# Zero products at the opening of a retention and rational feed-forward kernel: 59 of 64 columns and 3 long ones, in place of 93 in quarters of the array and 4 long ones

## The chip, the cores and the metric

The kernel runs on one core of a Trainium2 chip. The metric is the device time of one execution, in microseconds (us); smaller is better. Three runs of the kernel before are known: median 615.11 us, 614.29 to 615.46.

## What is computed

A retention layer (linear attention with a decaying state) feeds a feed-forward layer whose activation is a quotient of two polynomials. Cut to what matters:

```python
# q, k, v: (4, 8, 768, 64); w_in: (512, 2048); w_out: (2048, 512); a: 4 numbers, b: 2 numbers
gamma = 1.0 - 2.0 ** (-5.0 - np.arange(H))
for t in range(S):
    state = gamma[None, :, None, None] * state + np.einsum('bhd,bhe->bhde', k[:, :, t], v[:, :, t])
    y[:, :, t] = scale * np.einsum('bhd,bhde->bhe', q[:, :, t], state)
x = y.transpose(0, 2, 1, 3).reshape(B * S, H * D)          # 3072 x 512
h = x @ w_in
P = a[0] + a[1] * h + a[2] * h**2 + a[3] * h**3
Q = 1.0 + abs(b[0]) * abs(h) + abs(b[1]) * h**2
out = (P / (Q + 1e-06)) @ w_out
```

The zero products of this case are no part of it: TensorE multiplies a tile of zeros into a PSUM bank that nobody reads.

## The kernel before, in words

**Tiling.** The retention is done in chunks of 128 tokens: 4 batches by 6 chunks are 24 chunks. The first chunk of each batch (`first_chunk`, four calls) needs no state: its scores (`first_scores`, tile `pa`, L352) are k by q, VectorE multiplies them by the decay mask (tile `aT`, L541), and `first_values` (tile `px`, L358 and L366) multiplies by v. ScalarE and VectorE then split the result into a rounded high part and a rest (`xh`, L470, and `xl`, L474), since the large matrix products run as three products of such parts. The feed-forward layer goes over 6 blocks of 512 tokens and 16 slices of 128 hidden columns, 96 slots. In a slot TensorE makes `ph` (L827, 12 products of 512 columns), ScalarE, VectorE and GpSimd work out the quotient in some ten instructions, and TensorE adds to `po` (L846, 12 products).

**Weights.** They arrive as 64 bit numbers in 32 tiles `raw` of 512 KB each. `decode` turns each into a high part and a rest: two ScalarE instructions (tile `t`, L786, and tile `u`, L790), two on VectorE (L796, L799), a copy on ScalarE (L805) and a subtraction on GpSimd (L808). The first 16 or so are decoded while the first slots run.

**Order.** A planner written in the kernel (class `Plan`) orders all steps ahead of time from tables of costs and ranks; every engine then runs its list strictly in that order, and all loads and stores go through the one queue of SyncE (SP, L315) in that order. At most eight transfers are under way at once.

**The zeros.** When the planner finds a gap of over 0.7 us on TensorE, it puts zero products there. `fill` makes the long ones: 128 rows, 128 columns of weights, 512 columns streamed, bfloat16 (L291). Ahead of the very first step of TensorE, and only there, `open_with` runs (L303): 93 products of fp32 zeros, 64 by 64 weights and 16 streamed columns, by turns in two quarters of the array (`r = half(i % 2)` picks rows and output partitions 0 to 63 or 64 to 127); it then sets the number of long ones that follow, `BEGINNING`, to 4. The numbers do not enter the planner's times: it has fixed the order already when `open_with` runs. The tile `zeros` is a VectorE memset at the program's start (L259). The first step after the opening is the scores of one first chunk, then three long zeros, the scores of a second one, four long zeros, and the values of both.

Of the kernel before, what the change touches and what calls it, by code (L numbers as in the profile page):

```python
# [8 lines left out]
F32 = mybir.dt.float32  # L9
# [194 lines left out]
def tile_retention_rational_ffn(  # L204
# [22 lines left out]
    H, D = kk.shape[3], kk.shape[4]  # L227
# [26 lines left out]
    zeros = const.tile([P, P], BF16, name="zeros")  # L254
# [42 lines left out]
    def open_with(bank):  # L297


        few_ = zeros.bitcast(F32)  # L300
        for i in range(TURNING):
            r = half(i % 2)
            nc.tensor.matmul(  # L303
                bank[r, :16], few_[r], few_[r, :16], start=True, stop=True, skip_group_check=True
            )
        spare[0] = BEGINNING

# [19 lines left out]
    def half(x):  # L327
        return slice(x * D, (x + 1) * D)
# [704 lines left out]
    with tc.manual_schedule(  # L1033
# [45 lines left out]
        def emit(x, engine, gap):  # L1079

            nonlocal idle
            if engine == "PE" and zeros_for(gap):
                spare[0] = zeros_for(gap)
                if not begun(1):
                    if idle is None:
                        idle = ps.tile([P, TB], F32, name="idle", tag="b1")
                        open_with(idle)
                    fill(idle, True)
                elif open_po:
                    fill(open_po[0], False)  # L1090
            x.run(engine)
            spare[0] = 0
# [262 lines left out]
ENDING = (  # L1355
    (0, 0), (1, 0), (0, 1), (1, 1), (0, 2), (2, 0), (2, 1), (1, 2), (2, 2), (0, 3), (1, 3), (2, 3),
)
TURNING = 93
BEGINNING = 4


_ARRAYS = (
# [100 lines left out]
```

## Time and profile before

| | |
|---|---|
| median of 3 runs | 615.11 us (614.29 to 615.46) |
| the profiled execution | 615.57 us |
| its span, first to last instruction | 613.9 us |
| TensorE busy (products) | 605.4 us, 99% of the span |
| TensorE weight loads | 494.5 us, 81% |
| VectorE busy | 442.3 us, 72% |
| ScalarE busy | 429.8 us, 70% |
| GpSimd busy | 330.3 us, 54% |
| all DMA | 59.45 MB |

The profile is of one execution. PE stands for TensorE's products, PEld for its weight loads, DVE for VectorE, ACT for ScalarE, POOL for GpSimd, SPq for the DMA queue of SyncE. The zero products count as busy, so 99% says nothing of useful work. Of 615.57 us, 1.7 lie outside the span.

### The profile page before, as it was taken

The page shows a single profiled execution, that of the slowest core. Times are in us where ns is not written, and L with a number is a line of the kernel's source. Part 1 is how long each engine was busy: PE and PEld are TensorE (multiplying, and loading weights), DVE is VectorE, ACT ScalarE, POOL GpSimd, SP SyncE. Part 2 cuts the span into 40 slices and gives each one's busy share as a digit, 9 for nine tenths or more (in the row PEclk, how much of TensorE's full clock was granted, in tenths as well). Part 3 has the DMA queues.
Part 4 walks back from the last instruction along what each step waited for, and adds up shares of the span by engine and source line. Part 5 has one row for each costly group of instructions (what it writes and reads, how often), then busy time and mean ns, then how long its engine had stood idle before and what let it go on. Part 6 is the DMA issues. An engine that isn't in the chain of part 4 may idle for free.

```text
span 613.9 us, 13176 instructions
## 1 busy us (share of the span) xinstructions
PE 605.4 (99%) x5358; PEld 494.5 (81%) x5358; DVE 442.3 (72%) x665; ACT 429.8 (70%) x699; POOL 330.3 (54%) x276
## 2 busy tenths in 40 slices
PE   9998999999999999999999999999999999999997
PEld 7766888888888888888888888888888888888885
DVE  0699999898878868766677766666776666766664
ACT  1599989999855655756675775576775667777663
POOL 0478778786865655445544544444454344444442
PEclk9999999999999999999999999999999999999999
DMA  9999931001222470705003300400231000100001
GB/s 315 321 383 407 369 107 68 2 0 69 57 64 105 144 236 21 222 8 167 2 1 124 118 1 18 156 1 1 87 106 51 1 1 1 69 0 1 0 2 68
DMA packets 30412, 59.45 MB, mean 97 GB/s; under 512 B 3216, under 2 KB 8592, under 8 KB 30352
## 3 DMA queue, kind: packets, MB, share of 16 engines
q1 hardware_dynamic: 30352, 58.61, 26.9%
q8 instruction: 42, 0.69, 0.4%
q14 instruction: 18, 0.15, 0.1%
HBM read 50.21 MB, written 8.39 MB: 95 GB/s over the span
## 4 chain that ended last, share of the span: by engine, by line
PE 89%; DVE 0%; ACT 0%; issue 0%
PE po L846 42%; PE ph L827 41%; PE px L422 3%; PE pa L392 2%; PE pk L401 2%; DVE p L938 0%; DVE t L799 0%; DVE ph L937 0%; DVE q L936 0%; ACT o L993 0%
## 5 line engine op out<-in xcount | busy, mean ns | idle before, releaser
L909 POOL TENSOR_TENSOR q<-q,s 128x512 f32<-128x512 f32 x96 | 124.2, 1294 | 185.1 <-ACT s L898 170.3
L827 PE MATMUL ph<-xh,w 128*128 128x512 f32 (+2 forms) x776 | 208.3, 390 | 2.7 <-DVE p L938 1.4
L846 PE MATMUL po<-w,gh 128*128 128x512 f32 x768 | 199.5, 392 | 0.0
L827 PEld LDWEIGHTS ph<-xh,w 128*128 128x128 f32 x776 | 143.7, 188 | 33.7 <-ACT w L805 2.1
L846 PEld LDWEIGHTS po<-w,gh 128*128 128x128 f32 x768 | 143.0, 188 | 30.3
L936 DVE SCALAR_TENSOR_TENSOR q<-q,small,ph 128x512 f32<-128x512 f32 x96 | 71.7, 746 | 112.3 <-ACT ph L925 111.8
L948 POOL TENSOR_TENSOR gl<-p,gh 128x512 fp32r<-128x512 f32 x96 | 124.4, 1296 | 36.6 <-ACT gh L944 19.7
L924 ACT ACTIVATE s<-q,small 128x512 f32<-128x512 f32 x96 | 69.5, 724 | 64.9 <-POOL q L909 64.9
L846 PE MATMUL po<-w,gl 128*128 128x512 f32 x384 | 110.4, 390 | 0.0
L889 ACT ACTIVATE q<-ph 128x512 f32<-128x512 f32 x96 | 57.4, 598 | 69.3 <-PE ph L827 68.7
L827 PE MATMUL ph<-xl,w 128*128 128x512 f32 (+2 forms) x388 | 103.3, 388 | 0.0
L827 PEld LDWEIGHTS ph<-xl,w 128*128 128x128 f32 x388 | 72.6, 188 | 15.2
L846 PEld LDWEIGHTS po<-w,gl 128*128 128x128 f32 x384 | 72.0, 188 | 15.3 <-POOL gl L948 0.3
L904 ACT ACTIVATE p<-ph,small 128x512 f32<-128x512 f32 x96 | 74.5, 776 | 0.0
L918 DVE SCALAR_TENSOR_TENSOR p<-p,small,ph 128x512 f32<-128x512 f32 x96 | 71.7, 747 | 3.4
L917 DVE TENSOR_TENSOR p<-ph,p 128x512 f32<-128x512 f32 x96 | 65.7, 685 | 8.8 <-ACT p L904 8.4
L937 DVE SCALAR_TENSOR_TENSOR ph<-p,small,ph 128x512 f32<-128x512 f32 x96 | 71.9, 749 | 0.0
L938 DVE SCALAR_TENSOR_TENSOR p<-q,ph 128x512 f32<-128x512 f32 x96 | 65.9, 687 | 3.3
L944 ACT CAST gh<-p 128x512 fp32r<-128x512 f32 x96 | 59.1, 616 | 12.2 <-DVE p L938 12.0
L898 ACT ACTIVATE s<-q,small 128x512 f32<-128x512 f32 x80 | 65.0, 812 | 0.1
L925 ACT ACTIVATE ph<-s 128x512 f32<-128x512 f32 x96 | 57.8, 602 | 4.2 <-DVE p L918 0.9
L808 POOL TENSOR_TENSOR w<-t,w 128x512 fp32r<-128x512 f32 x32 | 41.4, 1297 | 30.4 <-ACT w L805 30.3
(59 smaller groups left out, 434.1 us busy)
## 6 DMA issues: line engine op xcount, KB each, us to landing
v<-in_v SPq DMA_DIRECT2D x34, 256.0 KB, 4.7
raw<-in_w_in SPq DMA_DIRECT2D x16, 512.0 KB, 9.0
raw<-in_w_out SPq DMA_DIRECT2D x16, 512.0 KB, 8.5
qT<-in_qT SPq DMA_DIRECT2D x24, 256.0 KB, 4.7
kT<-in_kT SPq DMA_DIRECT2D x24, 256.0 KB, 4.4
k<-in_k SPq DMA_DIRECT2D x24, 256.0 KB, 4.2
out<-o SPq DMA_DIRECT2D x24, 256.0 KB, 2.3
q2T<-in_q2T SPq DMA_DIRECT2D x10, 256.0 KB, 4.8
```

The source lines that it names most:

```text
L827: nc.tensor.matmul(cell["ph"][:, t0:t1], w[0, f][:, part, kt * P : (kt + 1) * P], x[:, kt, t0:t1], start=(i == 0), stop=(i == 3 * NP - 1),)
L846: nc.tensor.matmul(o_tiles[n][tt], g_[:, tt * P : (tt + 1) * P], w[1, f][:, part], start=(first and m == 0), stop=(last and m == 2),)
L898: nc.scalar.activation(cell["s"], cell["q"], AF.Identity, bias=babs[:, 0:1], scale=babs[:, 1:2])
L904: nc.scalar.activation(cell["p"], cell["ph"], AF.Identity, bias=par_sb[:, 2:3], scale=par_sb[:, 3:4])
L909: nc.gpsimd.tensor_mul(cell["q"], cell["q"], cell["s"])
L917: nc.vector.tensor_mul(p_, ph_, p_)
L918: nc.vector.scalar_tensor_tensor(ph_ if aside else p_, p_, par_sb[:, 1:2], ph_, ALU.add, ALU.mult)
L924: nc.scalar.activation(s_, cell["q"], AF.Abs_reciprocal_sqrt, bias=qcon[:, 0:1])
L936: nc.vector.scalar_tensor_tensor(q_, q_, qcon[:, 0:1], ph_, ALU.add, ALU.mult)
L937: nc.vector.scalar_tensor_tensor(ph_, p_, par_sb[:, 0:1], ph_, ALU.add, ALU.mult)
L938: nc.vector.scalar_tensor_tensor(p_, q_, 2.0, ph_, ALU.subtract, ALU.mult, reverse0=True)
L948: nc.gpsimd.tensor_sub(cell["gl"], cell["p"], cell["gh"].bitcast(F32))
```

## The change

`open_with` makes 59 products in place of 93. Each is a bfloat16 product of 128 rows, 64 columns of weights and 64 streamed columns, always at the same place (output partitions 0 to 63), instead of an fp32 product of 64 rows, 64 columns of weights and 16 streamed columns at two places by turns. The number of long zero products behind them goes from 4 to 3. Nothing else is changed.

```diff
     def open_with(bank):
 
 
-        few_ = zeros.bitcast(F32)
         for i in range(TURNING):
-            r = half(i % 2)
             nc.tensor.matmul(
-                bank[r, :16], few_[r], few_[r, :16], start=True, stop=True, skip_group_check=True
+                bank[:D, :D], zeros[:, :D], zeros[:, :D], start=True, stop=True, skip_group_check=True
             )
         spare[0] = BEGINNING
...
-TURNING = 93
-BEGINNING = 4
+TURNING = 59
+BEGINNING = 3
```

TensorE's list before, from the program's first instruction to the first scores (`idle` is the unread PSUM bank, 64x16 and 128x512 the output):

```order
L1459 UNCONDITIONAL_BRANCH
L303 MATMUL idle<-zeros 64x16 x93
L291 LDWEIGHTS zeros
L291 MATMUL idle<-zeros 128x512
L291 LDWEIGHTS zeros
L291 MATMUL idle<-zeros 128x512
L291 LDWEIGHTS zeros
L291 MATMUL idle<-zeros 128x512
L291 LDWEIGHTS zeros
L291 MATMUL idle<-zeros 128x512
L352 MATMUL pa<-qT,kT 64x128
```

The same place of the changed kernel, from the last of its 59 pairs of weight load and product (line numbers behind the edit are two lower):

```order
L301 LDWEIGHTS zeros
L301 MATMUL idle<-zeros 64x64
L291 LDWEIGHTS zeros
L291 MATMUL idle<-zeros 128x512
L291 LDWEIGHTS zeros
L291 MATMUL idle<-zeros 128x512
L291 LDWEIGHTS zeros
L291 MATMUL idle<-zeros 128x512
L350 MATMUL pa<-qT,kT 64x128
```

The 93 products before stand without rows for their weights because fp32 products get their loads only when the program is lowered: the trace shows two passes for each, 186 loads and 186 products. From the first scores on, TensorE's list and those of the other four engines are the same as before.

## Rows read from the trace of the kernel before

**Rows 1.** Stretches: busy us of each engine, granted clock, DMA share, GB/s.

```profile
25.60:61.60 36.00, 32.94 (x443) 24.73 (x440) 33.70 (x56) 34.03 (x59) 29.34 (x26) 1.00 1.00 379
61.60:613.90 552.30, 547.97 (x4460) 450.32 (x4460) 401.17 (x592) 389.24 (x628) 297.94 (x245) 1.00 0.20 68
```

**Rows 2.** The chain that ended last, around 61 us: start, length, what.

```profile
60.77 0.70 DVE p L938
61.47 0.14 issue
61.60 0.47 PE ph L827
```

**Rows 3.** Timeline of PE's products: start, length, line, operation, count, idle time before.

```profile
0.99 10.21 PE L303 MATMUL idle<-zeros 64*64 64x16 f32 x186 [0.99 <-DVE small L261]
11.12 1.89 PE L291 MATMUL idle<-zeros 128*128 128x512 bf16 x4
12.94 1.56 PE L352 MATMUL pa<-qT,kT 64*64 64x128 f32 x32
...
15.83 1.24 PE L352 MATMUL pa<-qT,kT 64*64 64x128 f32 x32
17.00 1.04 PE L291 MATMUL idle<-zeros 128*128 128x512 bf16 x4
17.97 0.69 PE L358 MATMUL px<-aT,v 64*64 64x64 f32 x16
```

**Rows 4.** Timeline of the weight loads of the long zeros.

```profile
11.53 0.15 PEld L291 LDWEIGHTS <-zeros 128*128 128x128 bf16 x1 [0.27 <-issue]
11.96 0.15 PEld L291 LDWEIGHTS <-zeros 128*128 128x128 bf16 x1 [0.28 <-issue]
```

**Rows 5.** Line L303: weight loads, ns min/median/max, first and last start.

```profile
L303 PEld LDWEIGHTS idle<-zeros x186: 178/223/228, 1.0 to 10.9; 64*64 64x64 f32 x186
```

**Rows 6.** Tile kT, window 1.5 to 3.4 us: two loads, issued at 1.6 and 3.0.

```profile
L315 SPq DMA_DIRECT2D kT<-in_kT x2: 423/428/432, 1.6 to 3.0; - x2
...
DMA to landing us min/median/max: 4.4/4.6/4.9
```

**Rows 7.** Tile first (the masks), window 3.9 to 4.9 us.

```profile
L315 SPq DMA_DIRECT2D first<-in_mask x2: 431/432/432, 4.0 to 4.5; - x2
...
DMA to landing us min/median/max: 4.5/4.8/5.0
```

**Rows 8.** Timeline of ACT and DVE in the first 23 us.

```profile
10.84 0.75 ACT L786 ACTIVATE t<-raw,small 128x512 uint32<-128x512 uint8 x1 [2.41 <-DMA raw<-in_w_in]
...
14.55 0.56 DVE L541 TENSOR_TENSOR aT<-pa,first 128x384 f32<-128x384 f32 x1 [13.60 <-PE pa L352]
...
17.13 1.49 DVE L541 TENSOR_TENSOR aT<-pa,first 128x384 f32<-128x384 f32 x3 [2.02 <-PE pa L352]
...
19.32 0.65 ACT L470 CAST xh<-px 128x256 fp32r<-128x256 f32 x2 [7.73 <-PE px L366]
...
22.59 0.78 ACT L786 ACTIVATE t<-raw,small 128x512 uint32<-128x512 uint8 x1
```

**Rows 9.** Tile raw, window 9.4 to 9.6 us: the second weight tile.

```profile
L315 SPq DMA_DIRECT2D raw<-in_w_in x1: 432/432/432, 9.5 to 9.5; - x1
...
DMA to landing us min/median/max: 6.3/6.3/6.3
```

**Rows 10.** Tile k, window 46.5 to 47 us: the later of two loads for a pair of chunks.

```profile
L315 SPq DMA_DIRECT2D k<-in_k x1: 517/517/517, 46.8 to 46.8; - x1
...
DMA to landing us min/median/max: 6.7/6.7/6.7
```

**Rows 11.** Timeline of POOL: the two instructions that read these two k tiles.

```profile
55.18 2.04 POOL L571 TENSOR_TENSOR k<-k,small 128x512 f32<-128x512 f32 x2
```

**Rows 12.** Two more stretches, columns as in rows 1.

```profile
24.50:31.00 6.50, 6.46 (x114) 6.04 (x111) 4.56 (x11) 5.24 (x11) 4.84 (x5) 1.00 0.81 267
37.00:57.00 20.00, 19.29 (x260) 13.46 (x260) 19.43 (x31) 19.31 (x34) 18.01 (x16) 1.00 1.04 407
```

## The prediction, made before the changed kernel was run

> **What bounds the kernel now.** I read the stretches first. From 61.6 us to the end TensorE is busy 547.97 of 552.30 us [rows 1], so that part cannot get shorter by anything done at the opening; it can only begin earlier. Between 25.6 and 61.6 us VectorE and ScalarE are busy 33.70 and 34.03 of 36.00 us [rows 1]: here the decoding of the weights sets the pace, and the chain of waits says the same, since VectorE's instructions hand over to TensorE at 61.6 us [rows 2]. Both engines run fixed lists. So the question is when these lists get going.
>
> The timeline of ACT and DVE answers it. ScalarE decodes one weight tile at 10.84 us, then stands idle for 7.73 us until the first values are there, at 19.32; VectorE stands idle for 13.60 us until the first scores end, and again 2.02 us for the second [rows 8]. The instructions behind these stand in line. All of them wait for TensorE, and TensorE is busy with zeros: the quarter products from 0.99 to 11.12 us, four long ones until 12.94 [rows 3].
>
> The data is not what it waits for. The two kT tiles are issued at 1.6 and 3.0 us and land 4.4 and 4.9 us later, at 6.0 and 7.95 (the qT before each is earlier in the same queue); the masks land at 8.5 and 9.5 [rows 6, 7]. The first scores could begin 6.9 us before they do. So the length of the zero stream is on the path that sets the end, microsecond for microsecond, until another thing is late.
>
> [...]
>
> **The change, step by step.**
>
> *Out: 93 quarter products.* They take 10.21 us, 0.110 each, or 0.055 for each of the 186 pairs of load and product [rows 3].
>
> *In: 59 products of 64 columns.* No such product is in the trace. A long zero streams 512 columns in 0.43 us, so 64 columns take 0.053. A load of 64 columns should need as long; the question is whether it runs beside the product before it. Of the long zeros it does: the loads start at 11.53 and 11.96, together with the product before [rows 4]. The nearest row, the pair of load and product in the quarters, gives 0.055 [rows 3]. I take 0.055: 59 x 0.055 = 3.25 us. Bounds: at the full clock half of that, 1.6 us; in series, load then product, what a whole quarter product takes, 0.110, or 6.5 us; and if each product had to wait until the record of its load ends, 0.223 [rows 5], 13.2 us.
>
> [...]
>
> *Three long zeros instead of four.* 0.43 us less: 1.28 instead of 1.71.
>
> *Where the first scores then stand.* The zeros end at 0.99 + 3.25 + 1.28 = 5.5 us. Now the data is late next: kT at 6.0. So the first scores start near 6.05 instead of 12.94, 6.9 us earlier; half a microsecond of the saving is already a wait.
>
> *From there to the values.* The second scores stand 2.89 us behind the first (15.83 - 12.94), at 8.95, and their kT has landed. VectorE's first mask product has its mask at 8.5; the next waits for the second scores, as now. If the clock is still low, these scores end at 10.45 and the four long zeros behind them last 1.71 us instead of 0.97: the values start near 12.25, 5.7 us earlier than the 17.97 of now. If the clock rises as far behind the start of the long zeros as now (11.12 to some point between 15.83 and 17.00, so 5 us or a little more), it does so near 9.6 and the values start near 11.35, 6.6 us earlier. I take 6.1.
>
> *What of it reaches the end.* The lists of VectorE and ScalarE start 6.1 us earlier, if their inputs come. The second weight tile lands at 9.5 + 6.3 = 15.8 and is read at 22.59 [rows 8, 9], 6.8 us of slack. The tightest that I found later is the k tile issued at 46.8: it lands at 53.5, and GpSimd reads it in the second half of the pair at 55.18, at 56.2 [rows 10, 11], 2.7 us of slack. The transfers must thus move by 3.4 us as well. They can: between 24.5 and 31 us they carry 267 GB/s where 407 is had from 37 to 57 [rows 12], (1 - 267/407) x 6.5 = 2.2 us of lost time, because the queue waits for buffers that TensorE and VectorE free; they would free them earlier, and a little more is lost outside this stretch. I charge 0.2 us for what stays.
>
> *Everything else* is the same list on every engine, and 254 fewer instructions in TensorE's opening cost nothing to anyone.
>
> Sum: 615.57 - 6.1 + 0.2 = 609.7 us on the scale of the profiled execution. That one was 0.46 above the median of the runs, so I predict **609.2 us**.
>
> **The rivals.**
>
> *Load and product in series.* 59 x 0.110 = 6.5 us: the opening shrinks by 10.21 - 6.5 + 0.43 = 4.1 us, all data is there, and the time is 611.0. For it: in the quarters a product with a 16-column stream still cost 0.110. Against it: rows 4. 0.17.
>
> *The clock rises early.* If the 64-column stream raises it, as the quarter stream did not, the second scores end near 9 us, the second mask at 9.5 plus a mask product of 0.56 lets the values start near 10.1, 7.9 us earlier, and the loads, tighter by that much, take back a part, an estimate of 0.8: 7.1 us, 608.0. [...] 0.12.
>
> *The loads hold.* If the transfers do not move, only the 2.7 us of slack at the k tile are gained there: 612.4. Against it: the lost time in rows 12. 0.05.
>
> *Slower: each product waits for its own load to end.* The quarters alternate between two places and the change has one. If the next load could start only when the product before is under way, and the product only when the load's record is over, each step costs 0.178 to 0.223 us [rows 5]. At 0.18 the opening is as long as now (59 x 0.18 = 10.6 = 10.21 + 0.43) and nothing changes, 615.1; this is the point from which it decides. At 0.223 it lasts 13.2 us, 2.5 longer: 617.6. Against it: of the quarters 186 such records fit into 10.21 us, so they overlap each other. 0.04 for about the same, 0.05 for slower. A gain eaten somewhere that I did not see adds 0.02 and 0.01.
>
> **How the numbers follow.** The forecast has 0.54, and with the series, the early clock and the loads that hold, which are all faster, 0.88. Same 0.06 and slower 0.06. The bound between them is 0.2%, 1.2 us, about what a measurement of this kernel tells from no change. The range reaches from the early clock with half a microsecond to spare, 607.5, past the series case to the loads that hold, 612.5; left out are the cases near 615 and above, and the edges.
>
> **What would show it.** Right: 59 products in about 3.3 us; the first scores at 6.0 to 6.2, with a short wait for kT; the values at 11 to 12.5; ScalarE's xh near 13; VectorE handing over to TensorE at 55 to 56 instead of 61.6; and the rest shifted as a whole. Wrong: products 0.11 us or more apart; the hand-over at 58 or later although the scores came early, with GpSimd or ScalarE waiting for k or raw; a clock that rises later than the start of the large products.

## The result, and the profile of the changed kernel

| | before | changed |
|---|---|---|
| median of five runs | 615.22 us (614.29 to 615.46) | 608.36 us (607.78 to 608.67) |
| the profiled execution, and its span | 615.57 us, 613.9 | 608.67 us, 607.0 |

The ratio is 0.9889, with a 95% interval of 0.9875 to 0.9904: faster by 6.9 us. Forecast were 609.2 us and a range of 607.5 to 612.5.

The timeline of TensorE's products in the changed kernel (start, length, line, operation, count, idle time before) answers to rows 3:

```profile
0.98 3.35 PE L301 MATMUL idle<-zeros 128*64 128x64 bf16 x59 [0.98 <-DVE small L261]
4.27 0.95 PE L291 MATMUL idle<-zeros 128*128 128x512 bf16 x3
6.58 0.90 PE L350 MATMUL pa<-qT,kT 64*64 64x128 f32 x32 [1.37 <-DMA kT<-in_kT]
7.42 0.82 PE L291 MATMUL idle<-zeros 128*128 128x512 bf16 x3
8.52 0.90 PE L350 MATMUL pa<-qT,kT 64*64 64x128 f32 x32 [0.28 <-DMA kT<-in_kT]
9.35 1.04 PE L291 MATMUL idle<-zeros 128*128 128x512 bf16 x4
10.32 0.79 PE L356 MATMUL px<-aT,v 64*64 64x64 f32 x16
...
12.66 0.77 PE L350 MATMUL pa<-qT,kT 64*64 64x128 f32 x24
14.03 0.45 PE L350 MATMUL pa<-qT,kT 64*64 64x64 f32 x8 [0.60 <-issue]
```

Three things stand in it. The 59 products take 3.29 us up to the next row, 0.056 each. The first scores wait 1.37 us for kT and then take 0.84 us up to the next row, where they took 1.50 before [rows 3]. Such durations are what low and high clock mean here: before, four long zeros took 1.82 us from 11.12 and 0.97 from 17.00, and the second scores 1.17, between 1.50 and 0.84 [rows 3], so the clock rose during these, between 15.83 and 17.00. In the changed kernel it is high at 6.6 us already, at least nine microseconds earlier. And the values start at 10.32 instead of 17.97 [rows 3], 7.65 us earlier. The last row shows something new, which the experiments turn out to be about: in the middle of a run of products TensorE stands still for 0.60 us and waits for nothing that the profile shows ("issue"). What it costs here no run shows by itself: with 0.34 us of it (e7) and with none (e11) the times are 608.28 and 607.89 us.

The timelines of ScalarE and of VectorE (rows 8 before):

```profile
10.80 0.77 ACT L784 ACTIVATE t<-raw,small 128x512 uint32<-128x512 uint8 x1 [1.96 <-DMA raw<-in_w_in]
11.77 0.65 ACT L468 CAST xh<-px 128x256 fp32r<-128x256 f32 x2 [0.20 <-PE px L364]
...
16.00 0.77 ACT L784 ACTIVATE t<-raw,small 128x512 uint32<-128x512 uint8 x1 [0.87 <-DMA raw<-in_w_in]
```

```profile
9.11 1.95 DVE L539 TENSOR_TENSOR aT<-pa,first 128x384 f32<-128x384 f32 x4 [8.17 <-DMA first<-in_mask]
13.73 0.69 DVE L797 SCALAR_TENSOR_TENSOR t<-raw,u 128x512 uint32<-128x512 uint32 x1
```

The long idle times in front of both lists are gone. VectorE's first mask product now waits for its mask and not for TensorE, and ScalarE's second weight tile, which had 6.8 us of slack, is waited for (0.87 us). So the loads have become the limit of the first 20 us. They take a part back: VectorE's first join of a decoded weight (L799 before, at 21.29; L797 now, at 13.73) is 7.56 us earlier, the third 7.14, and from the fourth on they are 6.95 earlier (6.88 at the last).

The chain of waits around the hand-over from VectorE to TensorE (rows 2), and the two stretches on either side (columns as in rows 1):

```profile
53.82 0.70 DVE p L936
54.52 0.14 issue
54.65 3.00 PE ph L825 x12
```

```profile
25.60:54.65 29.05, 26.16 (x347) 18.41 (x346) 28.20 (x46) 28.27 (x49) 24.57 (x22) 1.00 1.04 409
54.65:607.00 552.35, 548.01 (x4460) 450.63 (x4460) 401.23 (x592) 389.37 (x628) 297.92 (x245) 1.00 0.20 70
```

The hand-over is at 54.65 instead of 61.60, and the rest is the same: 552.35 us with 548.01 busy, where rows 1 have 552.30 and 547.97. All of the gain is made at the opening, less what the loads take back by 27 us (the fourth join), and carried to the end.

### The profile page after: what moved, and what is told of

Read it like the earlier page. It is cut to its first block, busy times and chain, and to the rows that moved or that the text cites. A ratio compares the mean times of both kernels' runs of the same rounds, so it can differ in the third digit from the quotient of the medians.

```text
span 607.0 us, 12921 instructions
## 1 busy us (share of the span) xinstructions
PE 596.5 (98%) x5230; PEld 486.5 (80%) x5230; DVE 442.4 (73%) x665; ACT 430.0 (71%) x699; POOL 330.4 (54%) x276
## 4 chain that ended last, share of the span: by engine, by line
PE 90%; DVE 0%; ACT 0%; issue 0%
PE po L844 43%; PE ph L825 41%; PE px L420 3%; PE pa L390 2%; PE pk L399 2%; DVE p L936 0%; DVE t L797 0%; DVE ph L935 0%; DVE q L934 0%; ACT o L991 0%
```

## The experiments

Three theories. **A**, that of the prediction: only the time at which the first scores and values start counts. **B**: the clock's early rise carries a good part of the gain. **C**, formed when A had failed in three of the first four runs (e2 to e4): the number of TensorE instructions ahead of the first scores counts by itself, because stalls stand at instructions that lie 256 or a multiple of it apart (e4 has the numbers), and the opening sets which of the later instructions these are. Such 256 instructions are called a block here, and their ends edges.

Counted are records of weight loads and products: a bfloat16 zero product is 2, a quarter product 4 (two passes of a load and a product), a long zero 2. Before: 93 x 4 + 4 x 2 = 380. Changed: 59 x 2 + 3 x 2 = 124. The difference is 256.

Each experiment sets the two numbers of the opening, in the new form (one place, 64 columns) or the old one (quarters, 16 columns). Median and difference are against the runs of before on the same chip (614.90 us for e1 to e4, 614.78 for e5 to e8, 615.22 for e9 to e11). Start of scores and values, span and stalls are of the profiled execution; the stalls are those of TensorE for "issue" behind the start of the values. "Rest" is the span less the start of the values.

| | form, products + long | count | scores | values | span | rest | stalls | median | difference | ratio (95%) |
|---|---|---|---|---|---|---|---|---|---|---|
| before | old, 93 + 4 | 380 | 12.94 | 17.97 | 613.9 | 595.9 | none | | | |
| changed | new, 59 + 3 | 124 | 6.58 | 10.32 | 607.0 | 596.7 | 0.60 | 608.36 | -6.9 | 0.9889 (0.9875 to 0.9904) |
| e1 | old, 30 + 3 | 126 | 6.62 | 12.82 | 608.4 | 595.6 | none | 609.04 | -5.9 | 0.9901 (0.9886 to 0.9915) |
| e2 | new, 300 + 4 | 608 | 13.21 | 17.38 | 613.2 | 595.8 | none | 615.12 | +0.2 | 1.0005 (0.9996 to 1.0013) |
| e3 | none | 0 | 6.73 | 12.83 | 611.1 | 598.3 | 1.89 | 611.64 | -3.3 | 0.9948 (0.9936 to 0.9959) |
| e4 | old, 60 + 4 | 248 | 9.32 | 14.18 | 612.9 | 598.7 | 1.52, 0.98 | 614.94 | 0.0 | 1.0002 (0.9992 to 1.0012) |
| e5 | new, 124 + 0 | 248 | 7.24 | 10.62 | 611.0 | 600.4 | 1.44, 0.38, 2.03 | 613.22 | -1.6 | 0.9984 (0.9972 to 0.9996) |
| e6 | new, 187 + 3 | 380 | 9.25 | 12.89 | 610.1 | 597.2 | 1.34 | 610.94 | -3.8 | 0.9937 (0.9925 to 0.9949) |
| e7 | new, 54 + 3 | 114 | 5.47 | 9.52 | 606.0 | 596.5 | 0.34 | 608.28 | -6.5 | 0.9894 (0.9882 to 0.9907) |
| e8 | old, 64 columns, 30 + 2 | 124 | 6.39 | 10.08 | 608.9 | 598.8 | none | 608.78 | -6.0 | 0.9905 (0.9892 to 0.9919) |
| e9 | new, 318 + 0 | 636 | 13.32 | 20.08 | 615.6 | 595.5 | none | 616.60 | +1.4 | 1.0026 (1.0016 to 1.0036) |
| e10 | old, 56 + 12 | 248 | 11.61 | 14.99 | 613.4 | 598.4 | 1.70, 0.45 | 616.32 | +1.1 | 1.0027 (1.0016 to 1.0038) |
| e11 | new, 36 + 5 | 82 | 5.29 | 9.04 | 606.0 | 597.0 | none | 607.89 | -7.3 | 0.9886 (0.9872 to 0.9899) |

The table is best read by its "rest". Without a stall behind 30 us it lies between 595.5 and 597.2 us, from whatever start; only e8 stands out, which is told of below. Where TensorE stalls later, it is 598.3 to 600.4.

### e1: short, but of the old kind

```diff
-TURNING = 93
-BEGINNING = 4
+TURNING = 30
+BEGINNING = 3
```

> The kernel before with 30 quarter products and 3 long zeros: the opening is as short as in the change, but made of the products after which the clock stayed low. Theory A (the start of the first scores is what counts, the clock adds a little): the zeros end at 0.99 + 30 x 0.110 + 3 x 0.43 = 5.6 us, the first scores wait for kT until 6.0 to 6.5 and run at the low clock (1.5 us), the clock rises near 10, the values start near 11.9 against 17.97 before and 10.32 in the change; time 609 to 609.5, against 615.2 before and 608.4 in the change. Theory B (the early clock is what counts): little is gained without it, 612 us or more.

Measured: 609.04 us, as A has it. The timeline of TensorE's products in e1:

```profile
0.98 3.38 PE L303 MATMUL idle<-zeros 64*64 64x16 f32 x60 [0.98 <-DVE small L261]
4.30 1.46 PE L291 MATMUL idle<-zeros 128*128 128x512 bf16 x3
6.62 1.56 PE L352 MATMUL pa<-qT,kT 64*64 64x128 f32 x32 [0.86 <-DMA kT<-in_kT]
8.11 1.46 PE L291 MATMUL idle<-zeros 128*128 128x512 bf16 x3
9.50 1.56 PE L352 MATMUL pa<-qT,kT 64*64 64x128 f32 x32
11.00 1.89 PE L291 MATMUL idle<-zeros 128*128 128x512 bf16 x4
12.82 0.46 PE L358 MATMUL px<-aT,v 64*64 64x64 f32 x16
```

The first scores start with those of the changed kernel, but the clock stays low: three long zeros last 1.46 us here and 0.95 there, and the values start 2.5 us later. Yet the medians differ by 0.7 to 1.0 us only (the profiled executions by 1.4). So 5.9 us of the 6.9 come from the shorter opening, and the clock brings about one; a part of what it gives is waited away for the loads, as seen above.

### e2: the new kind, as long as the old

```diff
-TURNING = 59
-BEGINNING = 3
+TURNING = 300
+BEGINNING = 4
```

> The changed kernel with 300 products of 64 columns and 4 long zeros: the opening is as long as before, but with the products during which the clock rose at about 4.5 us. At the 0.053 us that each took until then and an estimate of 0.03 at the full clock, the first scores start near 12.9 as before. Theory A: only the clock's part is gained: first scores 0.84 instead of 1.50 us, three zeros 0.65 instead of 1.39, second scores 0.8 instead of 1.17, so the values start about 1.3 us earlier than before, 16.7, and the time is 613.9. Theory B: most of the gain is there, 608 to 610.

Measured: 615.12 us, no difference, where A had 613.9. The values start 0.6 us ahead of those of before, with the clock high ahead of the scores (46 zeros take 1.62 us from 7.82, 0.035 each, against 0.056 for the 59 of the changed kernel; the first scores take 0.83); two stalls for "issue", 0.28 us among the zeros and 0.37 among the scores, lie in front of them. So an early clock behind an opening as long as before gained nothing; what it would bring without these two stalls e2 does not show.

### e3: no zeros at all

```diff
-TURNING = 59
-BEGINNING = 3
+TURNING = 0
+BEGINNING = 0
```

> The changed kernel with no products in the opening at all (0 and 0); TensorE stands until kT lands at 6.0 to 6.5 us. Theory A: the scores start there at the low clock, the values start near 12.2 (5.7 us earlier than before), time 609.5, about 1 us above the change: the zeros are worth only what the clock is. Theory B: the clock rises some 5 us after the first scores, after most of the opening's work; 612 us or more.

Measured: 611.64 us. This is a miss: scores and values start as in e1, and the time is 2.6 us longer. VectorE's and ScalarE's lists run 5.0 us ahead of before up to 40 us. Then the timeline of TensorE's products shows this, and the stretches behind it (columns as in rows 1) what follows:

```profile
40.05 0.22 PE L420 MATMUL px<-q2T,state 64*64 64x64 f32 x1
42.15 0.21 PE L420 MATMUL px<-qT,state 64*64 64x64 f32 x1 [1.89 <-issue]
...
43.11 1.84 PE L825 MATMUL ph<-xh,w 128*128 128x512 f32 x4
```

```profile
40.00:42.20 2.20, 0.31 (x21) 0.18 (x14) 1.67 (x3) 1.95 (x4) 1.28 (x1) 1.00 1.00 393
42.20:43.40 1.20, 1.20 (x52) 1.13 (x52) 0.18 (x1) 0.45 (x1) 0.84 (x1) 1.00 1.01 413
43.40:46.80 3.40, 3.40 (x9) 2.68 (x9) 3.31 (x6) 2.34 (x4) 2.87 (x4) 0.50 1.03 400
```

TensorE stalls for 1.89 us in the middle of the short products of L420, little more than a microsecond later the granted clock is at 0.50 for 3.4 us, and the end keeps 2.7 us of the 5.0 gained.

### e4: half as far with the old kind

```diff
-TURNING = 93
+TURNING = 60
```

> The kernel before with 60 quarter products instead of 93 and the same 4 long zeros. Theory A: 33 x 0.110 = 3.6 us go from the opening, the first scores start at 9.3 with their data there, everything behind them keeps its distance, and the time is 615.2 - 3.6 = 611.6, microsecond for microsecond. Theory B: no gain without the clock, 614.5 or more.

Measured: 614.94 us, no difference to before: A's worst miss, for scores and values start 3.6 and 3.8 us earlier, and VectorE's joins are 3.8 us earlier until 40 us. The timeline shows where most of it goes:

```profile
41.31 0.22 PE L422 MATMUL px<-q2T,mid 64*64 64x64 f32 x1
43.05 0.21 PE L422 MATMUL px<-q2T,mid 64*64 64x64 f32 x1 [1.52 <-issue]
...
71.89 0.41 PE L422 MATMUL px<-aT,v 64*64 64x64 f32 x15
73.28 0.50 PE L422 MATMUL px<-aT,v 64*64 64x64 f32 x17 [0.98 <-issue]
```

At the last join 1.0 us of the 3.8 is left in this execution, which at 614.58 us lies a little under the median of the twelve (613.84 to 617.73); what the others lost no trace shows.

The kernel before has no stall for "issue" between 36 and 82 us. Counted along all of TensorE's records, its few waits for semaphores included, the stall at 41.3 stands in front of instruction 1474 and that at 72.3 in front of 2242; the one of e3 stands in front of 1218, the one in the changed kernel's scores in front of 450. These lie 256 or a multiple of it apart. That is theory C. The packets of instructions agree with these distances: TensorE's records number 10790 before and 10534 in the changed kernel, 42.1 and 41.1 times 256, and queue q8 carries 42 packets (0.69 MB) and 41 (0.67 MB), each of 16 KB.

### e5: the start of the changed kernel, with another count

```diff
-TURNING = 59
-BEGINNING = 3
+TURNING = 124
+BEGINNING = 0
```

> The changed kernel with 124 products of 64 columns and no long zeros: the zeros still end before kT lands (67 products at 0.053 until the clock rises near 4.5 us, the rest at 0.03: 6.2 us), so the scores start as in the change, but TensorE's list holds 248 instructions ahead of them (load and product each count one; a quarter product counts four) instead of 124, as many as in the kernel with 60 quarters that gained nothing. Theory C (instructions come in blocks of 256, 16 KB, and TensorE stands at a block's edge where its instructions are short; before and change differ by exactly one block, 380 and 124): stalls of 1 to 1.5 us within the values near 37 and 66 us, time 610.5 to 611.5. Theory A (the start of the scores alone counts): 608.4, as the change.

Measured: 613.22 us, 1.6 us faster than before instead of 6.9: C, and by more than I had put. The first scores start at 7.24, the values at 10.62, and VectorE's joins come 0.2 to 0.4 us behind those of the changed kernel at first and 0.03 us behind them from the fourth on, until 36 us. Then:

```profile
38.19 0.22 PE L420 MATMUL px<-q2T,mid 64*64 64x64 f32 x1
39.84 0.21 PE L420 MATMUL px<-q2T,mid 64*64 64x64 f32 x1 [1.44 <-issue]
...
68.98 0.41 PE L420 MATMUL px<-aT,v 64*64 64x64 f32 x15
71.42 0.50 PE L420 MATMUL px<-aT,v 64*64 64x64 f32 x17 [2.03 <-issue]
```

These are the same two instructions as in e4, with the same split of 15 and 17 products, in a kernel that is otherwise 3 us earlier: the place goes with the count, 248 in both, and not with the time. After the first of them the joins are 1.2 us later than in the changed kernel, at the end 4.1. The transfers between 37.3 and 37.7 us of e5 show what comes ahead of the stall's end (queue, kind: packets, MB, share of 16 engines):

```profile
q8 instruction: 1, 0.02, 13.7%
```

One packet of instructions starts there, and the stall ends some 2.3 us behind it. In every stall of TensorE's products for "issue" in the traces, such a packet of queue q8 starts 2.2 to 2.6 us ahead of the stall's end (in the changed kernel at 11.65, 2.4 us ahead of 14.03).

### e6: one block more than the changed kernel

```diff
-TURNING = 59
+TURNING = 187
```

> The changed kernel with 187 products of 64 columns and 3 long zeros: 380 instructions, as many as before and one block more than the change. The opening ends near 8.8 us, about 2.2 us later than the first scores of the change and a little earlier than those of the 60 quarters (9.32), which ran as long as before. Theory C: no new stalls, the later start costs 2.2 us less some slack at the loads, 610 to 610.6. Theory A as it was put for the 60 quarters predicts the same; if something holds every start between 7 and 13 us to the time of before, 614 to 615.

Measured: 610.94 us. The scores start at 9.25, as late as e4's 9.32 within 0.1 us, and the time is 3.9 us shorter, each taken against its own runs of before. From the fourth to the seventh join of a decoded weight (30.3 to 39.0 us) VectorE is ahead of before by 3.74 us in e6 and by 3.79 in e4. So both are equally far there; e6 keeps its lead to the last join (3.80), and e4 loses most of its own at the two stalls. A count of 256 more leaves every later edge in its place: no stall in L420. The old edge in the third scores costs more here, 1.34 us at 15.89, where it cost 0.60.

### e7: fewer of the new kind

```diff
-TURNING = 59
+TURNING = 54
```

> The changed kernel with 54 products instead of 59: 10 instructions fewer, so the edge of the block at which TensorE stood 0.60 us within the third scores (13.43 to 14.03) moves into the six long zeros behind them. The scores start as in the change, since kT sets them. Theory C: that stall goes; the loads take most of it back, 608.0 to 608.4, unless another edge now meets short instructions. Theory A: 608.4.

Measured: 608.28 us, a ratio of 0.9894, not to be told from the changed kernel. The stall did not go: 0.34 us of it are left, three products ahead of the end of the third scores, where it was eight in the changed kernel. Ten instructions move the edge by five products only, so the run does not price that stall. In this execution kT landed 3.7 us behind its issue (4.8 in the changed kernel's) and the first scores started at 5.47, still at the low clock (1.49 us up to the next row).

### e8: quarters, but with 64 columns

```diff
-                bank[r, :16], few_[r], few_[r, :16], start=True, stop=True, skip_group_check=True
+                bank[r, :D], few_[r], few_[r, :D], start=True, stop=True, skip_group_check=True
...
-TURNING = 93
-BEGINNING = 4
+TURNING = 30
+BEGINNING = 2
```

> 30 quarter products that stream 64 columns of fp32 instead of 16, and 2 long zeros: 124 instructions as in the change, the opening about as long, in quarters of the array as before. If the quarters as such leave the clock low: first scores at the low clock, clock near 12, 609.0 as with the 30 short quarters. If the longer streams are what raises it: clock near 4.5 to 8 us, 608.4 as the change.

Measured: 608.78 us (607.58 to 610.68). Its timeline:

```profile
0.99 3.47 PE L303 MATMUL idle<-zeros 64*64 64x64 f32 x60 [0.99 <-DVE small L261]
...
6.39 0.90 PE L352 MATMUL pa<-qT,kT 64*64 64x128 f32 x32 [1.14 <-DMA kT<-in_kT]
```

The pairs cost 0.057 us, no more than with 16 columns, and the clock is high at the first scores (0.84 us up to the next row). Against e1, with as many quarter products and a count of 126 beside 124, only the columns that are streamed differ, and one long zero. So neither the quarters of the array nor fp32 alone kept the clock low in e1. The profiled execution was the slowest of the five: a third kT came 1.2 us late, TensorE waited 2.04 us for a decoded weight until 52.2, and the granted clock was 0.51 from 52.7 to 56.2, which makes its "rest" long.

### e9: long, with the count of before

```diff
-TURNING = 59
-BEGINNING = 3
+TURNING = 318
+BEGINNING = 0
```

> The changed kernel with 318 products of 64 columns and no long zeros: 636 instructions, two blocks of 256 more than the 124 of the change, so the edges stay where they were. The first scores start near 12.9 us as before, at the full clock. This prices the clock alone. Theory A with C: the values start some 1.3 us earlier than before, 613.5 to 614.3 (615.1 with 300 and 4, whose count was off by 28). If the early clock were the main part: 608 to 610.

Measured: 616.60 us, slower than before, where no loss was expected. Modulo 256 its count is that of before, and indeed no later stall shows. What I had left out is that the edges within the opening count too. The timeline and the stretches (columns as in rows 1):

```profile
14.15 0.39 PE L291 MATMUL idle<-zeros 128*128 128x512 bf16 x1
16.18 0.97 PE L291 MATMUL idle<-zeros 128*128 128x512 bf16 x2 [1.64 <-issue]
17.09 1.56 PE L350 MATMUL pa<-qT,kT 64*64 64x128 f32 x32
```

```profile
12.00:14.50 2.50, 2.50 (x77) 2.12 (x74) 0.23 (x1) 0.00 (x0) 0.00 (x0) 1.00 1.04 397
14.50:16.20 1.70, 0.06 (x2) 0.02 (x2) 0.33 (x1) 0.00 (x0) 0.00 (x0) 1.00 1.03 386
16.20:20.20 4.00, 4.00 (x44) 2.01 (x48) 1.49 (x3) 0.00 (x0) 0.00 (x0) 0.57 0.68 236
```

Instruction 706 is a long zero behind the first scores here. TensorE stalls 1.64 us in front of it, the clock falls to 0.57, and the values start at 20.08, 2.1 us later than before. From there on it is the kernel before (rest 595.5). So e9, like e2, does not price the clock alone.

### e10: earlier than before, with a bad count

```diff
-TURNING = 93
-BEGINNING = 4
+TURNING = 56
+BEGINNING = 12
```

> The kernel before with 56 quarter products and 12 long zeros: the opening is about as long (56 x 0.110 + 12 x 0.43 = 11.3 us against 11.9), but holds 248 instructions instead of 380, as in the two kernels that stalled within the values. Theory C: stalls of 1 to 2 us near 43 and 74 us; in spite of a start 0.6 us or more earlier it is slower than before, 617 to 618.5. Theory A: 614 to 614.6.

Measured: 616.32 us, slower than before, although the values start 3.0 us earlier: as C has it in sign, with a smaller loss. The profiled execution, at 615.07, was the fastest of eleven, so its stalls are less than what the median lost. A third kernel with 248, and the first stall is at the same instruction as in e4 and e5:

```profile
42.18 0.22 PE L422 MATMUL px<-q2T,mid 64*64 64x64 f32 x1
44.10 0.21 PE L422 MATMUL px<-q2T,mid 64*64 64x64 f32 x1 [1.70 <-issue]
```

### e11: shorter still

```diff
-TURNING = 59
-BEGINNING = 3
+TURNING = 36
+BEGINNING = 5
```

> The changed kernel with 36 products of 64 columns and 5 long zeros: 82 instructions, 42 fewer than the change, so that the edge that stood within the third scores falls into the six long zeros behind them or later. The zeros end near 5.1 us, before kT lands. Theory C: the stall of 0.6 us there goes, 607.5 to 608.3; or another edge meets short instructions and it is slower than the change, 609 or more. Theory A: 608.4.

Measured: 607.89 us (607.75 to 608.52). The first scores start at 5.29, 1.3 us earlier than in the changed kernel, and the rest is 597.0. But the zeros end no earlier: near 5.3 here, near 5.2 in the changed kernel, which then waits 1.37 us for kT. In this execution kT landed 3.2 us behind its issue, in that one 4.8. So the earlier start comes from the landing and not from the edit. This is the shortest median of all, by half a microsecond, but the two ratios overlap: it is no proven gain over the change.

## Why the prediction was right, and where it was not

**The zeros on the path: right.** 59 products came to 3.29 us where 3.25 were put, 0.056 each for 0.055, and the opening's end lies ahead of the data. That the length counts is what e1 shows: with the old products, cut to the same length, 5.9 of the 6.9 us come.

**Load and product side by side: right**, and the series rival is out. Line L301 of the changed kernel, loads and products (ns min/median/max):

```profile
L301 PEld LDWEIGHTS <-zeros x59: 126/157/158, 1.0 to 4.0; 128*64 128x64 bf16 x59
L301 PE MATMUL idle<-zeros x59: 241/241/260, 1.0 to 4.1; 128*64 128x64 bf16 x59
```

Records of 157 and 241 ns that follow each other every 56 lie on top of one another. In series, at 0.110 each, the step would have cost 3.2 us more; the measurement decides against it here. That a load takes as long as the stream of 64 columns was my estimate; how long one takes by itself no run shows. The slower rival, a product that waits for its load's record, falls with the same rows.

**"The first scores start near 6.05": half a microsecond too early.** They wait for kT until 6.58. The landing of this tile is not fixed: scores that waited for it or started when it was there began at 5.29 (e11), 5.47 (e7), 6.39 (e8), 6.62 (e1) and 6.73 us (e3). The second kT and the first mask were late too: the second scores wait 0.28 us for kT until 8.52 and the mask product starts at 9.11, where 7.95 and 8.5 were put.

**"I take 6.1" for the shift of the values: the term that was mis-sized.** It was 7.65. Two sums behind the 6.1 do not come out as written: 10.45 + 1.71 is 12.16 and not 12.25, and with the lengths of before (1.17 and 0.97) the second case gives 8.95 + 1.17 + 0.97 = 11.1 and not 11.35. Put right they give shifts of 5.8 and 6.9, so the larger part of the miss is not there. I had put the clock's rise at 9.6 us or later, by the time that it took behind the long zeros before. No run shows that this time is fixed: in e1 the long zeros begin at 4.30, and those from 11.00 to 12.82 still take 0.46 each. Here the clock was high by 6.6 us, so the second scores came 1.94 us behind the first instead of 2.89, and the four long zeros took 0.97 instead of 1.71. That is the rival to which I gave 0.12: values 7.9 us earlier, 0.8 taken back by the loads, 608.0 us in all. Measured were 7.65, 0.70 (7.65 - 6.95) and 608.36. I gave it little because the trace had ten microseconds of products and the clock low behind them [rows 3]. That did not tell what this opening would do; of two openings as short, e1 shows the clock low behind its quarter products (first scores 1.49 us up to the next row) and e8 shows it high (0.84). My forecast of 609.2 describes e1, with the low clock, which took 609.04.

The signs that the prediction named for itself say the same: the values came at 10.32 (11 to 12.5 was put), ScalarE's xh at 11.77 (near 13), the hand-over at 54.65 (55 to 56). All three lie on the side of the early clock. The path was right; the case that happened was the rival's, and that the number is still near is in part luck.

**"I charge 0.2 us" for the loads: 0.70.** The second weight tile, with 6.8 us of slack, is the one that runs out, as it had to at a shift of more than that. The recovery of lost transfer time is borne out: the stretch from 25.6 us to the hand-over moves 409 GB/s, where it moved 379 before [rows 1].

**"254 fewer instructions in TensorE's opening cost nothing to anyone": true by the number alone.** With the long zero it is 256, and it holds for that number and not for any. With 248 ahead of the scores, three kernels lost 2 to 4 us of stalls between 38 and 74 us, and e4 lost its whole gain. Of e5 my sum would have put the first scores at 0.99 + 124 x 0.055 = 7.8 us, 5.1 earlier than before; they came at 7.24, and of the gain 1.6 us were left. In the prediction nothing stood for this: that the change takes away exactly one block was luck.

**The sum.** Shift 6.1 less 0.2 was put; 7.65 less 0.70 came. The two errors, 1.55 and 0.50, partly cancel: a gain of 5.9 us was put and one of 6.9 measured, and the time came out 0.8 us below the forecast.

## What to carry to other kernels

A filler ahead of work that waits for data should end when the data lands; look for the engine behind it that stands idle, and ask what is late next. If instructions are added to or taken from the front of an engine's straight program, count them: where a change of count moved the edges of the instruction blocks into runs of short products, 2 to 4 us of stalls came that no wait in the trace explains (e4, e5, e10), and "issue" in the middle of a run is the mark to look for. Where the number can be chosen, change it by a whole block, 256 here (e6: no stall in L420), or try several.

## What was not expected of the hardware

**Block edges.** Stalls of the products for "issue" of 0.3 to 2.0 us stand at TensorE's instructions 450, 706, 1218, 1474, 1986 and 2242 of these programs, all 194 plus multiples of 256, and only at some of the edges: the changed kernel passes 1218 and 1986 in the products of L420 without one. In the stalls the packet of instructions started 2.1 to 4.8 us behind the edge before (in the changed kernel 4.0, 11.65 behind 7.64). Later in the program, where the DMA share is 0.20, blocks of under 5 us went by with no stall (before, from 240.45 to 244.34 us, at a share of 0.21). Why TensorE stalls at some edges and not at others no run shows. The kernels with 248 ahead of the scores also vary more: their 11 or 12 executions spread over 3.2 to 3.9 us (e4, e5, e10), where the 11 of e2 spread over 2.2.

**What ran before the clock rose.** Before the change, quarter products with 16 columns ran back to back for 10.2 us, and the clock was still low behind them (four long zeros in 1.82 us from 11.12); so it was behind the short opening of e1 (three in 1.39 from 8.11). In the kernels with 64 columns in the opening, in quarters of the array or not, it was high by 8 us at the latest: the first scores take 0.84 us up to the next row at 6.58 in the changed kernel and at 6.39 in e8, and 0.83 at 7.24 in e5; three long zeros take 0.76 from 6.96 in e7 and end within 0.82 from 6.33 in e11; 135 of the products take 4.72 us from 3.78 in e6, a mean of 0.035; e9 has 67 products from 6 to 8 us and 23 from 5 to 6; e2 is told of above. That is what the traces show of these openings, and no rule.

**A stall can cost twice.** After stalls of 1.64 us (e9) and 1.89 us (e3), and after e8's wait of 2.04, the granted clock fell to 0.50 to 0.57 for 3 to 4 us; after 2.03 us (e5: 1.00 from 71.42 to 75.00) and 1.70 us (e10: four products of L827 in 1.03 us from 44.96, where those in e3 took 1.64 from 43.11) it did not. What decides it stays open. In the opening, where durations show the low clock, that column reads 1.00 (e1, from 8 to 12 us, with three long zeros in 1.39): there the clock has to be read from the time of a known product.
